# A linear-attention and feed-forward kernel: one-piece state update, operand sums shared with GpSimd, a second burst for Gram and query products

## The chip, the cores and the metric

The kernel runs on one core of a Trainium2 chip. The metric is the device time of one execution in microseconds (us); smaller is better. PE is TensorE (matrix products), DVE is VectorE, ACT is ScalarE, POOL is GpSimd, SP is SyncE. All data is float32.

## The reference

Two parts follow each other. The first is a delta-rule recurrence over 768 tokens, for 4 batches of 8 heads with 48 dimensions each; the second is a feed-forward layer on its output, seen as 3072 tokens of 384 features.

```python
k_n = k / (norm(k) + 1e-6)
state = 0                                   # 48 x 48 for each batch and head
for t in range(768):
    y[t] = q[t] @ state
    v_old = state.T @ k_n[t]
    state = state + beta[t] * outer(k_n[t], v[t] - v_old)
x = y.transpose(0, 2, 1, 3).reshape(3072, 384)
h = x @ w_in                                # 384 x 2048
g = maximum(h, 0) + alpha * minimum(h, 0)
out = g @ w_out                             # 2048 x 384
```

## The kernel before, in words

**Attention.** The tokens are cut into 12 chunks of C = 64 (NCH = 12), the batches into two pairs, which gives N = 24 steps n, one for a chunk and a pair of batches. Within a chunk the recurrence becomes a triangular system: the Gram products of the keys (`grams`, L527 and the DVE work L535 behind it) make the matrix, DVE eliminates in small blocks (`eliminate`, L606 and L612, for four steps at a time), PE combines the blocks (`between`, L788 and L800), `solve` (L958, then u at L962 on DVE) gives u of a step, `outputs` (L971) adds to its y, `query` (L836, copied at L840 by ACT) prepares the products of queries and keys, and `next_state` updates the state. `next_state` (L981 to L1001) writes its product for the two heads of a pair at rows 0 to 47 and 64 to 111 of a PSUM bank; DVE subtracts them from the state at L995, in two operations of 48 rows. For the first steps (n < 8, with exceptions) there is a form of 128 rows, one operation. Gram products run 9 steps ahead of the step that needs them, query products one step ahead. `to_ffn` (L1003) turns y by PE transposes and ACT copies it to `xt` (L1014), the input of the feed-forward part.

**Feed-forward.** It works on chunks of 256 tokens, 12 of them. Chunks 0 and 1 are ordinary products. For chunk 2 the second product, and from chunk 3 on both, take a form of Strassen's scheme with seven half-size products instead of eight, for which sums of the operands are made ahead:

- `input_sums` (L1260 to L1272, GpSimd) makes sums of w_in once; `token_sums` (L1295 to L1306, DVE, four operations of 128 x 128) makes sums of the chunk's tokens, needed by its first products at L1360.
- `ffn_in_fast` (from L1310) runs the first product in 8 groups of two blocks. For each group `common` (L1373) ends the shared products, ACT copies them to `sums` (L1379), GpSimd makes three additions (L1384), DVE adds the group's own products (`total`, L1388, writes `act`), ACT applies the negative branch (L1394, L1397) and DVE adds it (L1401 or L1404).
- `operand_sums` (L1061 to L1071, DVE) makes from `act` the four operand sums of the second product, for the first four groups (`first`) and the last four (`rest`): s1 and s2, then a21 (in place in `act`), then s4. A count of the matrix products issued (class `Due`, L1274) sets where in the order each of them comes. In chunks 3 to 7 (`some` in the code, c < ALL = 8) they are due late, some of them during the second product.
- `ffn_out_faster` (from L1459) runs the second product, p[0] to p[6] in PE's order (L1484), with additions into `o_sb` by DVE (L1480). `ffn_out_fast` is the same for chunk 2.

The feed-forward of chunk c can start when attention steps 2c and 2c + 1 are done; it is the filling between the attention's small products from step 6 on.

**Order.** The order of instructions on each engine is the program's order (L203); there is no scheduler behind it. From step n = JOINED = 6, each step has three stretches (L2082). In a stretch, first a burst of small attention products is issued at once; then the generators of the stretch are interleaved by their shares (`weave`): some 12 pieces of feed-forward, pieces of elimination, and a list `later` of what is left of the burst. `later` is spread over the part of the stretch that is left from a share `soon` on (0.5 is the second half). The three stretches begin with

1. `burst_a` (L1576): outputs and state update of step n - 1, the product of step n's queries or keys with the state;
2. `turn_round` (L1620): `to_ffn` of step n - 1, and at every second step `token_sums` of the next feed-forward chunk (L1626), and transposes for later steps;
3. `burst_b` (L1604): `solve(n)`, the Gram products of step n + 9, the query products of step n + 1 and the block products of `between`, all in one burst on PE, with the work on their results on DVE and ACT behind it.

Constants of the conditions: EARLY = 8, LATE = 16 (from there no Gram products are left), ASK = 8, SOME = 3, NJ = 4; `ends` is true where n % 4 == 2, when an elimination has to be ended.

Of the kernel before, what the change touches and what calls it, by code (L numbers as in the profile page):

```python
# [32 lines left out]
C = 64  # L33
# [12 lines left out]
def kernel(  # L46
# [62 lines left out]
    def dims(i):  # L109
        return slice(64 * i, 64 * i + D)  # L110
# [870 lines left out]
    def next_state(n, p=None):  # L981
        c, bp = steps[n]
        pieces, wide = [], n < 2 * NJ and n not in late_keys
        if c < NCH - 1:
            p = region(p, G * D, g=G)
            for g, a, t in quarters():
                nc.tensor.matmul(
                    p[half(a) if wide else dims(a), t, g], late_key(n)[half(t ^ a), 2 * g + a, 0 : C if wide else D],
                    us[n][half(t ^ a), a, g],
                )  # L990


            def less(rows):
                x = state[bp][rows]
                nc.vector.tensor_tensor(out=x, in0=x, in1=p[rows], op=ALU.subtract)  # L995

            if wide:
                pieces = [lambda: less(slice(0, 2 * C))]
            else:
                pieces = [lambda: less(dims(0)), lambda: less(dims(1))]  # L1000
        return pieces  # L1001

    def to_ffn(n, p=None):  # L1003
# [54 lines left out]
            i, flat = i - 6, more.rearrange("p i s e -> p (i s e)")  # L1058
        return flat[:, i * 512 : (i + 1) * 512].rearrange("p (f i) -> p f i", f=2)

    def operand_sums(b):  # L1061

        x = act[:, 4 * b : 4 * b + 4].rearrange("p i f (u e) -> p i f u e", u=2)
        a11, a12, a21, a22 = x[:, :, 0, 0], x[:, :, 1, 0], x[:, :, 0, 1], x[:, :, 1, 1]
        s1, s2, s4 = (sums[:, 4 * b : 4 * b + 4, i] for i in range(3))
        for dst, x, y, op in (
            (s1, a21, a22, ALU.add), (s2, s1, a11, ALU.subtract), (a21, a11, a21, ALU.subtract),
            (s4, a12, s2, ALU.subtract),
        ):
            nc.vector.tensor_tensor(out=dst, in0=x, in1=y, op=op)  # L1070
            yield  # L1071

    w_half = w_out.rearrange("p (i f) (v e) -> p i f v e", f=2, v=2)
# [95 lines left out]
    def ffn_out_fast(c):  # L1169
# [53 lines left out]
        add(o[0][:, right_], o[0][:, right_], p)  # L1223
        store(c, 0, o[0])
        yield
        p = yield from product(operand(1, 1), w_sum_(3))
        add(o[1][:, left], u[1], p)
        store(c, 1, o[1])
# [81 lines left out]
    def ffn_in_fast(c):  # L1310
# [97 lines left out]

            return own, common, total, below, slope

        first, rest = operand_sums(0), operand_sums(1)
        two_z = [beyond_sums[:, :, 1], beyond_sums[:, :, 2]]

        def run(gen):
# [44 lines left out]
    def ffn_out_faster(c):  # L1459
# [52 lines left out]
        last = c == NCH - 1  # L1512
        if last:
            store(c, 0, o[0], left)
        yield from some(p[6], sum_(2), weight(1, 1), range(FP - 2))
        assert c + 1 == NCH or c + 1 in whole
        yield from some(p[6], sum_(2), weight(1, 1), range(FP - 2, FP))
        add(o[0][:, right_], o[0][:, right_], p[6])
        store(c, 0, o[0], right_ if last else slice(0, DM))
# [84 lines left out]
    def burst_b(n):  # L1604

        b, x = ps_big(), ps_big()
        soon = solve(n, b[:, :, 0:WY])
        gram = grams(n + EARLY + 1, x[:, :, 0 : G * C])
        asked = query(n + 1, x[:, :, G * C : G * C + WY]) if n + 1 >= ASK else []
        wanted = [(n + 1, True, b[:, :, WY : WY + G * HB])]  # L1610
        if n > JOINED:
            wanted.append((n + 2, False, b[:, :, 2 * WY : 2 * WY + G * HB]))
        soon += between(*wanted)
        if n >= LATE:
            now(soon[:1])
            return soon[1:] + asked
        now(soon + gram[:2] + asked)
        return gram[2:] + [lambda: (squares if n < ONE else squared)(n + EARLY + 2)]

    def turn_round(n):  # L1620

        after = n > ASK and n % 2 == 1
        if n > JOINED and not after:
            to_ffn(n - 1)
            if n >= 2 * SOME + 2:
                token_sums(n // 2 - 1)  # L1626
        flips(n + EARLY + 1, n + 2)
        later = weigh(n + EARLY + 1)
        if after:
            later.append(lambda: to_ffn(n - 1))  # L1630
        load_next(n)
        load_q(n + 3)
        return later
# [472 lines left out]
    for n in range(JOINED, N):  # L2106
# [26 lines left out]
        if n == JOINED:  # L2133
            stretch(fill[2], blocks, share[2], later, *extra[2])
            for _ in blocks:
                assert False
            place(n + 2, (0,))
            place(n + 3, (0,))
            blocks = eliminate(m)
        else:  # L2140
            if ends:
                blocks = eliminate(m) if m < N // NJ else iter(())
            after = [(placing(n + 2, (1, 2, 3)), PLACING)]
            if n % NJ != 1:
                after.append((placing(n + 3, (0,)), 1))
            if n >= LATE:
                put_off, after = after, []
            stretch(
                fill[2], blocks, share[2], later, *after, *extra[2], soon=0.1 if n >= LATE or ends else 0.5
            )  # L2150
    stretch(12, iter(()), 0, burst_a(N))
    to_ffn(N - 1)
    token_sums(NCH - 1)
    for _ in tail:
        pass

# [29 lines left out]
```

## Time and profile before

| what | value |
|---|---|
| time, median of 3 runs | 649.26 us |
| the three runs | 650.35, 647.86, 649.26 us |
| time of the profiled execution | 649.88 us |
| its span in the profile | 648.1 us |
| mean granted clock of TensorE | 0.995 of full |
| stretch of the feed-forward chunks 3 to 7 in the trace | 220 to 470 us |

In the page's rows of engines, each engine's busy time is given with its share of the span and its count of instructions; PEld is the loading of weights, which lies beside PE's work. The chain of waits (fourth part) follows the work that ended last back to its start and gives shares of the span. In a row of the timeline stand the start, the duration (both us), the engine, the line, the operation, the tiles (out<-in), the shape and the number of instructions in the row; what is in brackets behind is the idle time of the engine ahead of it and what ended it. In a row of the windows stand the stretch and its length, then busy time with its count of instructions for PE, PEld, DVE, ACT and POOL, then three figures: the granted clock, the busy share of the DMA engines and their rate in GB/s. In a row of the waits stand the waiting instruction, its releaser, the sum of idle time, the count and the longest.

### The profile page before, as it was taken

Reading aid. Unit: us, or ns where it says so; the run is one execution under the profiler, and the core shown is the slowest. Engines: PE = TensorE matmul, PEld = TensorE weight load, DVE = VectorE, ACT = ScalarE, POOL = GpSimd, SP = SyncE. Lnnn points to the kernel's source line nnn. Section 1 sums busy time; section 2 is a strip of 40 time slices with the busy share of each in tenths; the row PEclk is TensorE's granted clock in tenths of the full one; section 3 lists DMA queues with packets and bytes.
Section 4 is the critical chain, followed back from the end, with each engine's and each line's share of the span. In section 5 each row is a group of like instructions: output and inputs, shape, how many; then the busy total and the mean of one; then the engine's idle time right before and its main releaser. Section 6 shows DMA issues by size and latency. Waiting matters only on the chain.

```text
span 648.1 us, 22180 instructions
## 1 busy us (share of the span) xinstructions
PE 631.2 (97%) x9387; PEld 566.5 (87%) x9387; DVE 500.5 (77%) x1182; ACT 307.2 (47%) x710; POOL 200.8 (31%) x377
## 2 busy tenths in 40 slices
PE   8989999999999999999999999999999999999997
PEld 7777777566889989999898989999999999999997
DVE  5868689978998799678969849969958568467383
ACT  6776754245554286287178167157145055042240
POOL 7267610010071241152051044044044053062360
PEclk9999999999999999999999989999999999999999
DMA  8756965113301320311311201121111210100000
GB/s 129 199 152 162 253 141 128 24 28 67 71 16 26 75 50 3 74 33 22 64 33 31 47 24 34 25 50 27 33 45 27 47 31 2 34 17 2 26 1 24
DMA packets 106803, 36.93 MB, mean 57 GB/s; under 512 B 99872, under 2 KB 103088, under 8 KB 106704
## 3 DMA queue, kind: packets, MB, share of 16 engines
q1 hardware_dynamic: 104832, 35.03, 25.0%
q8 instruction: 73, 1.20, 0.8%
q10 hardware_dynamic: 1872, 0.49, 0.4%
q14 instruction: 26, 0.21, 0.1%
HBM read 30.78 MB, written 4.72 MB: 55 GB/s over the span
## 4 chain that ended last, share of the span: by engine, by line
PE 71%; DVE 15%; issue 7%; ACT 3%; DMA 2%; POOL 1%; DVEq 0%; POOLq 0%; ACTq 0%
PE p_more L1484 12%; PE p_ffn L1484 8%; PE p_more L1360 5%; PE p_ffn L1159 5%; PE p_ffn L1350 4%; PE p_more L1350 4%; PE p_ffn L1116 3%; PE p_ffn L1355 3%; PE p_ffn L1181 3%; PE p_more L1355 3%; PE p_ffn L1360 3%; PE p_pair L788 2%; DVE prod L606 2%; PE p_pair L848 2%; PE p_pair L471 2%
## 5 line engine op out<-in xcount | busy, mean ns | idle before, releaser
L1384 POOL TENSOR_TENSOR sums<-sums 128x128 f32<-128x128 f32 (+1 forms) x201 | 119.8, 598 | 291.2 <-ACT sums L1379 280.5
L1116 PE MATMUL p_ffn<-xt,w_in 128*128 128x256 f32 x288 | 69.7, 389 | 2.1 <-ACT act L1126 1.2
L1116 PEld LDWEIGHTS p_ffn<-xt,w_in 128*128 128x128 f32 x288 | 52.2, 190 | 11.0 <-ACT act L1126 1.6
L1014 ACT COPY xt<-p_pair 128x384 f32<-128x384 f32 x22 | 10.4, 476 | 105.5 <-PE p_pair L1010 81.6
L612 DVE TENSOR_TENSOR block<-block,prod 128x30 f32<-128x30 f32 (+9 forms) x150 | 52.7, 351 | 5.2
L606 DVE TENSOR_TENSOR prod<-block 128x30 f32<-128x30 f32 (+9 forms) x150 | 51.9, 346 | 4.5 <-POOL block L596 2.7
L1484 PE MATMUL p_more<-w_out,act 128*128 128x192 f32 x288 | 52.1, 329 | 0.0
L1484 PEld LDWEIGHTS p_more<-w_out,act 128*128 128x128 f32 x288 | 47.0, 190 | 0.4
L1379 ACT COPY sums<-p_more 128x512 f32<-128x512 f32 x44 | 25.7, 583 | 40.3 <-PE p_more L1360 37.3
L1350 PE MATMUL p_ffn<-xt,w_in 128*128 128x256 f32 x140 | 43.2, 391 | 0.1
L1350 PE MATMUL p_more<-xt,w_in 128*128 128x256 f32 x128 | 38.9, 386 | 2.1 <-DVE act L1388 2.1
L962 DVE TENSOR_TENSOR u<-p_pair,wgt 128x384 f32<-128x384 f32 x20 | 11.1, 554 | 35.1 <-PE p_pair L788 35.1
L800 ACT COPY inv<-p_pair 32x256 f32<-32x256 f32 x40 | 14.5, 362 | 34.1 <-DVE u L962 33.3
L1388 DVE TENSOR_TENSOR act<-p_ffn,sums 128x512 f32<-128x512 f32 x35 | 23.8, 681 | 7.0 <-POOL sums L1384 3.5
L1379 ACT COPY sums<-p_ffn 128x512 f32<-128x512 f32 x23 | 13.4, 582 | 33.4 <-PE p_ffn L1360 33.1
L1394 ACT ACTIVATE a_t<-act 128x512 f32<-128x512 f32 x31 | 19.5, 631 | 17.3 <-DVE act L1388 17.1
L460 POOL TENSOR_TENSOR beta_t<-beta_t,rec 128x8 f32<-128x8 f32 x20 | 5.1, 254 | 72.4 <-DVE rec L454 65.8
L1388 DVE TENSOR_TENSOR act<-p_more,sums 128x512 f32<-128x512 f32 x32 | 21.7, 679 | 6.7 <-POOL sums L1384 6.5
L1484 PE MATMUL p_ffn<-w_out,act 128*128 128x192 f32 x144 | 26.4, 326 | 0.0
L1484 PE MATMUL p_more<-w_out,sums 128*128 128x192 f32 x144 | 24.9, 326 | 0.0
L1484 PEld LDWEIGHTS p_ffn<-w_out,act 128*128 128x128 f32 x144 | 23.9, 190 | 0.0
L1355 PEld LDWEIGHTS p_ffn<-xt,w_in 128*128 128x128 f32 x140 | 21.6, 195 | 1.9
(327 smaller groups left out, 1698.3 us busy)
## 6 DMA issues: line engine op xcount, KB each, us to landing
v_raw<-in_v_dram SPq DMA_DIRECT2D x48, 96.0 KB, 2.8
qp<-in_q_dram SPq DMA_DIRECT2D x48, 96.0 KB, 2.9
out_dram<-o_sb SPq DMA_DIRECT2D x90, 48.0 KB, 1.6
space_out<-in_moe_w_out_dram SPq DMA_DIRECT2D x11, 384.0 KB, 4.1
ke<-in_k_dram SPq DMA_DIRECT2D x43, 96.0 KB, 3.2
kl<-in_k_dram SPq DMA_DIRECT2D x80, 48.0 KB, 2.5
w_out<-in_moe_w_in_dram SPq DMA_DIRECT2D x6, 512.0 KB, 4.6
w_out<-in_moe_w_out_dram SPq DMA_DIRECT2D x5, 384.0 KB, 4.1
```

What stands on the lines that cost most here:

```text
L606: nc.vector.tensor_tensor(out=prod, in0=r[:, 0:j, j : j + 1].to_broadcast([128, j, n]), in1=r[:, j : j + 1, j + 1 : HB].to_broadcast([128, ...
L612: nc.vector.tensor_tensor(out=r[:, 0:j, j + 1 : HB], in0=r[:, 0:j, j + 1 : HB], in1=prod, op=ALU.add)
L1116: nc.tensor.matmul(p_h[:, i], w_in[:, t, (f + i) * 128 : (f + i + 1) * 128], xt[:, t], start=(t == 0), stop=(t == KT - 1),)
L1159: nc.tensor.matmul(p_o[u], gs[f // 2][:, f % 2, u * 128 : (u + 1) * 128], w_out[:, f], start=(f == 0), stop=(f == FT - 1),)
L1350: nc.tensor.matmul(p[:, f * 256 : f * 256 + 256], w(2, f), xt[:, 2], start=True, stop=False)
L1355: nc.tensor.matmul(p[:, j * 128 : j * 128 + 128], a, b, start=False, stop=(j > 0))
L1360: nc.tensor.matmul(q[:, j], a, b, start=True, stop=True)
L1379: nc.scalar.copy(z, q)
L1384: nc.gpsimd.tensor_tensor(out=dst, in0=a, in1=b, op=ALU.add)
L1388: nc.vector.tensor_tensor(out=g.rearrange("p f (u e) -> p (f u) e", u=2), in0=p.rearrange("p (i e) -> p i e", e=128), in1=z, op=ALU.add,)
L1394: nc.scalar.activation(r, g, ACT.Relu, scale=-1.0)
L1484: nc.tensor.matmul(p, x(i), w(i), start=(i == 0), stop=(i == FP - 1))
```

## The change

1. `next_state`: one subtraction over rows 0 to 111 instead of two over 48 rows. Rows 48 to 63 between the two heads are subtracted too; nothing reads them.
2. `operand_sums`: in chunks 3 to 7 the last two of four sums (a21 and s4), of `first` and of `rest`, go to GpSimd. There are 20 such operations.
3. `token_sums` of the next chunk is issued in the second product: in `ffn_out_fast` ahead of the last product, in `ffn_out_faster` behind the two additions of p[5], ahead of p[6]. It is taken out of `turn_round` and out of the end.
4. `burst_b`: for n = 8 to 14 the Gram products and the query products leave the burst and are issued as a burst of their own, as the first piece of `later`. For n from 16 on no Gram product was or is issued.
5. The share from which `later` is spread in the third stretch: 0.0 instead of 0.1 where `ends` and n is 8 to 15, 0.1 instead of 0.5 for the other n from 8 to 15.

Compared instruction by instruction, PE's order differs by the 7 places where 16 + 16 small products (L527 and L836) move behind some large ones; DVE's 16 pairs of state updates become 16 single ones and its 20 sums go to POOL; the token sums stand earlier or later by some instructions; on ACT some copies (L840, L572, L427, L741) change places; SP's order is the same.

```diff
@@ next_state
-                pieces = [lambda: less(dims(0)), lambda: less(dims(1))]
+                pieces = [lambda: less(slice(0, C + D))]
@@ operand_sums
-    def operand_sums(b):
+    def operand_sums(b, engine=nc.vector):
...
-        for dst, x, y, op in (
+        for i, (dst, x, y, op) in enumerate((
             (s1, a21, a22, ALU.add), (s2, s1, a11, ALU.subtract), (a21, a11, a21, ALU.subtract),
             (s4, a12, s2, ALU.subtract),
-        ):
-            nc.vector.tensor_tensor(out=dst, in0=x, in1=y, op=op)
+        )):
+            (nc.vector if i < 2 else engine).tensor_tensor(out=dst, in0=x, in1=y, op=op)
             yield
@@ ffn_out_fast
         yield
+        assert c + 1 in whole
+        token_sums(c + 1)
         p = yield from product(operand(1, 1), w_sum_(3))
@@ ffn_in_fast
-        first, rest = operand_sums(0), operand_sums(1)
+        engine = nc.gpsimd if some else nc.vector
+        first, rest = operand_sums(0, engine), operand_sums(1, engine)
@@ ffn_out_faster
+        if not last:
+            assert c + 1 in whole
+            token_sums(c + 1)
         yield from some(p[6], sum_(2), weight(1, 1), range(FP - 2))
@@ burst_b
-        gram = grams(n + EARLY + 1, x[:, :, 0 : G * C])
-        asked = query(n + 1, x[:, :, G * C : G * C + WY]) if n + 1 >= ASK else []
...
+        if ASK <= n < LATE - 1:
+
+            def second():
+                gram, asked = other()
+                rest[:] = gram[2:]
+                now(gram[:2] + asked)
+
+            rest = []
+            now(soon + between(*wanted))
+            return [second, lambda: now(rest), lambda: squared(n + EARLY + 2)]
+
+        gram, asked = other()
@@ turn_round
             to_ffn(n - 1)
-            if n >= 2 * SOME + 2:
-                token_sums(n // 2 - 1)
@@ the loop over the steps
-                fill[2], blocks, share[2], later, *after, *extra[2], soon=0.1 if n >= LATE or ends else 0.5
+                fill[2], blocks, share[2], later, *after, *extra[2], soon=0.0 if ends and ASK <= n < LATE else 0.1 if n >= ASK or ends else 0.5
             )
     stretch(12, iter(()), 0, burst_a(N))
     to_ffn(N - 1)
-    token_sums(NCH - 1)
```

`other()` makes the Gram products (for n below 16) and the query products (for n from 7 on) as before.

More of the change, by code (lines that the diff above doesn't have):

```diff
@@ L1514, in ffn_out_faster @@
             store(c, 0, o[0], left)
+        if not last:
+            assert c + 1 in whole
+            token_sums(c + 1)
         yield from some(p[6], sum_(2), weight(1, 1), range(FP - 2))
-        assert c + 1 == NCH or c + 1 in whole
         yield from some(p[6], sum_(2), weight(1, 1), range(FP - 2, FP))
@@ L1612, in burst_b, with other @@
             wanted.append((n + 2, False, b[:, :, 2 * WY : 2 * WY + G * HB]))
+        def other():
+            gram = grams(n + EARLY + 1, x[:, :, 0 : G * C]) if n < LATE else []
+            asked = query(n + 1, x[:, :, G * C : G * C + WY]) if n + 1 >= ASK else []
+            return gram, asked
+        if ASK <= n < LATE - 1:
[7 more added lines that the diff above has]
+        gram, asked = other()
         soon += between(*wanted)
```

## The prediction

> **What bounds the kernel now.** I read the first and fourth part of the page, then the waits of PE over 216 to 648 us, then the timeline at each of them.
>
> ```profile
> span 648.1 us, 22180 instructions
> PE 631.2 (97%) x9387; PEld 566.5 (87%) x9387; DVE 500.5 (77%) x1182; ACT 307.2 (47%) x710; POOL 200.8 (31%) x377
> PE 71%; DVE 15%; issue 7%; ACT 3%; DMA 2%; POOL 1%; DVEq 0%; POOLq 0%; ACTq 0%
> ```
>
> ```profile
> PE p_more L1350 <- DVE act L1388: 2.1, 2, 1.3
> ```
>
> PE is busy in 97% of the span. The change takes no matrix product away, so PE's 631 us of work stay; it can gain only by shortening waits. In the 432 us that it touches, PE waits for DVE in the two places of this row and once at a seam between chunks, and once for no partner that the profile shows. The timeline has the four, the idle time in brackets (1.28 + 1.24 + 0.86 = 3.4 us behind DVE):
>
> ```profile
> 242.59 0.70 PE L1350 MATMUL p_more<-xt,w_in 128*128 128x256 f32 x2 [1.28 <-DVE act L1388]
> 321.34 0.46 PE L1360 MATMUL p_ffn<-xt,w_in 128*128 128x128 f32 x2 [1.24 <-DVE o_sb L1480]
> 343.14 0.70 PE L1350 MATMUL p_more<-xt,w_in 128*128 128x256 f32 x2 [0.86 <-DVE act L1388]
> 378.54 0.25 PE L788 MATMUL p_pair<-diag,right 32*32 32x32 f32 x3 [1.39 <-issue]
> ```
>
> Two lie in the input products of chunks 3 and 5, one at the seam between chunks 4 and 5. Behind the fourth the granted clock falls (the third figure from the end of each row):
>
> ```profile
> 378.00:380.00 2.00, 1.46 (x12) 1.42 (x12) 1.18 (x4) 0.57 (x2) 0.00 (x0) 0.89 0.03 8
> 380.00:382.00 2.00, 2.00 (x9) 1.73 (x8) 0.64 (x2) 1.95 (x6) 0.00 (x0) 0.50 0.00 0
> 382.00:384.00 2.00, 2.00 (x13) 1.90 (x12) 0.53 (x1) 1.94 (x6) 1.17 (x3) 0.76 0.00 0
> ```
>
> The lost clock is 2 x 0.11 + 2 x 0.50 + 2 x 0.24 = 1.7 us, so this stall costs 3.1 us in all; nothing in the change touches it.
>
> **The state update.** Two subtractions of 48 rows become one of 112 rows. The trace has the pair and a one-piece form of 128 rows:
>
> ```profile
> 189.78 0.54 DVE L995 TENSOR_TENSOR beside<-beside,p_pair 128x384 f32<-128x384 f32 x1
> 259.51 1.11 DVE L995 TENSOR_TENSOR beside<-beside,p_pair 48x384 f32<-48x384 f32 x2
> ```
>
> So each of 16 updates frees 0.57 us of DVE. What that is worth at the waits comes below.
>
> **Two of four operand sums on GpSimd.** In chunks 3 to 7, four L1070 operations a chunk leave DVE. Each is 0.68 us long and 0.60 us from its start to the next one's:
>
> ```profile
> 252.56 0.68 DVE L1070 TENSOR_TENSOR sums<-sums,act 128x512 f32<-128x512 f32 x1
> 253.16 0.33 DVE L606 TENSOR_TENSOR prod<-block 128x168 f32<-128x168 f32 x1
> ```
>
> DVE is rid of 4 x 0.60 = 2.4 us a chunk. GpSimd needs 1.3 us for such an operation, and the two engines hold each other up:
>
> ```profile
> 178.56 1.27 POOL L1272 TENSOR_TENSOR ke<-w_in 128x512 f32<-128x512 f32 x1
> 179.91 1.32 POOL L1272 TENSOR_TENSOR ke<-ke,w_in 128x512 f32<-128x512 f32 x1
> 181.20 2.04 POOL L1272 TENSOR_TENSOR qp<-w_in 128x512 f32<-128x512 f32 x1
> ```
>
> ```profile
> 179.24 0.64 DVE L606 TENSOR_TENSOR prod<-block 128x30 f32<-128x30 f32 x1
> 179.92 0.21 DVE L612 TENSOR_TENSOR block<-block,prod 128x30 f32<-128x30 f32 x1
> 180.04 0.55 DVE L962 TENSOR_TENSOR u<-p_pair,wgt 128x384 f32<-128x384 f32 x1
> 181.16 0.95 DVE L1103 TENSOR_TENSOR w_out<-w_out,space_out 128x768 f32<-128x768 f32 x1
> ```
>
> L606 takes 0.64 us, against 0.21 for its twin L612 just behind, and ends when GpSimd's first operation does. L962, with one operand in PSUM, passes unhindered. L1103 came first, and GpSimd's third operation took 2.04 us. So whoever starts first goes through, and the other waits if DVE reads both operands from SBUF.
>
> The Trainium skill, "SBUF — State Buffer", section "Who interferes with whom", speaks against this edit: a DVE instruction with two SBUF inputs and a GpSimd instruction that reads SBUF exclude each other for a whole instruction, and issue order decides who blocks. The trace agrees (0.64 against 0.21 us). By that rule alone a moved sum may cost DVE its whole length; that is the slower rival.
>
> DVE's own business there is elimination (L606, L612), both operands in SBUF, each waiting for the one before, so that GpSimd slips in between; and three of the four moved operations become ready behind one another. Let D be how much later DVE reaches the end of a chunk. If GpSimd blocks nothing, D = -2.4 - 0.6 = -3.0 us. If each blocks its full 1.3 us, D = 5.2 - 3.0 = +2.2 us. I take 1.1 us each (the first runs partly beside additions with a PSUM operand), near the row of 0.64, which lost the whole rest: D = 4.5 - 3.0 = +1.5 us.
>
> GpSimd's queue bears it: its next work, the first L1384 of the following chunk, comes after 26.62 us of idleness (the two small L460 and L461 stand ahead of it).
>
> ```profile
> 272.73 1.79 POOL L1384 TENSOR_TENSOR sums<-sums 128x128 f32<-128x128 f32 x3 [26.62 <-ACT sums L1379]
> 261.93 1.46 PE L1484 MATMUL p_ffn<-space_out,act 128*128 128x192 f32 x8
> 268.33 2.77 PE L1484 MATMUL p_more<-w_out,sums 128*128 128x192 f32 x16
> ```
>
> PE reads the moved results from 261.93 (act) and 268.33 us on (sums). The last input of GpSimd's chain, the L1070 of 252.56, is there at 253.2. Three operations of 1.3 us, with DVE's 0.7 us between, are through by 259.2: hidden, with 2.7 us to spare. Without that cover, a late result would stall PE one for one.
>
> **The token sums**, moved behind the two additions that free PE's bank. At the seam of chunk 4:
>
> ```profile
> 319.58 0.28 DVE L1306 TENSOR_TENSOR sums<-xt 128x128 f32<-128x128 f32 x1
> 320.58 0.61 DVE L1480 TENSOR_TENSOR o_sb<-u,p_ffn 128x192 f32<-128x192 f32 x2
> 321.63 0.39 PE L1360 MATMUL p_ffn<-sums,ke 128*128 128x128 f32 x2
> ```
>
> PE's first product of the next chunk needs the bank (free at 321.19), its second the second token sum. In the new order the additions run at 319.58 + D, the second sum ends at 320.77 + D, and that second product starts 0.15 us later, at 320.92 + D, against 321.63: the stall changes by D - 0.7, at best by -1.24. Behind the additions on DVE wait only these sums and transposes. The seam of chunk 6 has little room too:
>
> ```profile
> 420.36 0.29 DVE L1306 TENSOR_TENSOR sums<-xt 128x128 f32<-128x128 f32 x1
> 422.55 0.39 PE L1360 MATMUL p_ffn<-sums,ke 128*128 128x128 f32 x2
> ```
>
> There the second product could start at 420.36 + 1.34 + D = 421.70 + D against 422.55: D - 0.85, at best 0. At D = 1.5 the seams cost 0.8 + 0.65 = **+1.5 us** (bounds: -1.2 at D = -3.0, +2.9 at +2.2). The seams of 3, 5 and 7 I cost at nothing, by that of 3:
>
> ```profile
> 268.17 0.29 DVE L1306 TENSOR_TENSOR sums<-xt 128x128 f32<-128x128 f32 x1 [0.54 <-ACT xt L1014]
> 270.93 0.38 PE L1360 MATMUL p_ffn<-xt,w_in 128*128 128x128 f32 x2
> ```
>
> DVE idles there for 0.54 us before the token sums; with the additions behind them (1.0 + 0.6 us) it is through at 269.8, 1.1 us ahead of PE.
>
> **The waits of 242.59 and 343.14** end with an L1388 (241.87, below) in a DVE stretch without gaps, and each has one shortened state update ahead of it. At most 0.57 us each comes through; part is lost because ACT and GpSimd work ahead of the same L1388. I take 0.45 each, **-0.9 us** (bounds: 0, and -2.1 if both waits go).
>
> ```profile
> 241.87 0.67 DVE L1388 TENSOR_TENSOR act<-p_more,sums 128x512 f32<-128x512 f32 x1
> 240.00:242.00 2.00, 1.32 (x10) 1.05 (x8) 1.97 (x5) 1.97 (x6) 0.63 (x1) 1.00 0.75 133
> ```
>
> **A second burst.** For n = 8 to 14, Gram and query products move behind the other small ones, after a few large products: seven more changes between large and small tiles. The old burst:
>
> ```profile
> 223.22 0.39 PE L1360 MATMUL p_ffn<-sums,ke 128*128 128x128 f32 x2
> 223.53 0.68 PE L958 MATMUL p_pair<-r,inv 64*64 64x48 f32 x32
> 224.03 0.66 PE L527 MATMUL p_pair<-k_t 48*64 48x64 f32 x32
> 225.76 0.49 PE L1360 MATMUL p_more<-xt,w_in 128*128 128x128 f32 x2
> 586.83 0.68 PE L958 MATMUL p_pair<-r,inv 64*64 64x48 f32 x32
> 587.44 0.76 PE L1484 MATMUL p_more<-w_out,act 128*128 128x192 f32 x3
> ```
>
> Products like 223.22 follow each other every 0.22 us, so entering costs 223.53 - 223.44 = 0.1 us. The same 32 small products take 0.50 us inside the burst (223.53 to 224.03) and 0.61 us when large ones follow (586.83 to 587.44): leaving costs 0.1 us more than going on. An additional burst is thus 0.2 us, 7 x 0.2 = **+1.4 us** (bounds: 0.5 if the seams inside the old burst, now gone, pay most of it; 2.8 at twice the price). In return u (L962) is released about 1 us earlier; the L535 that need the Gram product still hold DVE until the second burst ends, so I cost this at nothing. The ACT copies that move (L572, L840, L427) stand in another order ahead of the same L1379, with the same sum within 0.3 us. The share that starts pieces earlier (0.0, 0.1 for 0.5) only makes these moves; no DMA changes place on its queue.
>
> **Sum.** The profiled execution took 649.88 us (span 648.1 and 1.8 around it), 0.62 above the median 649.26. +1.5 - 0.9 + 1.4 = +2.0 gives 651.9 on its account, and **651.2 us** beside the median.
>
> **Rivals.**
>
> *DVE first at the port, faster.* With D = -2 or less the stall of 321.34 goes (-1.24), and 242.59 and 343.14 go with it (-2.1); the bursts cost 0.5 to 1.4. 649.88 - 3.3 + 1.0 = 647.6, 647.0 beside the median. For it: L1103 at 181.16. Against it: L606 at 179.24.
>
> *GpSimd blocks DVE in full, slower.* D = +2.2: seams +2.9, bursts +1.4, nothing gained in the input products: 654.2 on the profile's account. A seam stall of 1.24 + 1.5 = 2.7 us is twice the one that halved the clock; another 1.7 us would give 655.9. In the middle, and beside the median: 654.4 us. It decides against the change from D of about 1.6 us (seams 1.65 + bursts 1.4 - 0.9 = 2.2) on, past 0.5% from D of about 2. For it: the two-operand rows. Against it: DVE has PSUM work to put beside.
>
> The Trainium skill, "TensorE: Matmul & The Clock Gate", section "Why this matters for your kernels", lets the clock fall only after idle gaps of about 3 us; here it fell to 0.50 after 1.39 us, and not after 1.28, so length alone does not settle it. By that page the slower rival would stay without the extra 1.7 us.
>
> *The stall of 378.54 is not tied to this code.* It waits for nothing shown; if it falls elsewhere or away, the forecast loses up to 3.1 us: 648.1 beside the median. For it: the three runs before span 647.86 to 650.35.
>
> *The edits do not reach PE.* If DVE's relief and GpSimd's blocking cancel (D near 0.7), only the bursts show: 650.1.
>
> **How the numbers follow.** Forecast 651.2 (649 to 652.5) 0.40; edits that do not reach PE, 0.08; DVE first, 0.16; stall moved, 0.08; GpSimd blocks in full, 0.28. About 0.5% (3.25 us: 646.0 to 652.5) is what a measurement can tell here. Faster by more needs DVE first together with the stall gone, or the cheap bound of the bursts: 0.14. Slower by more: the blocking rival and a tail of the forecast: 0.32. Within: 0.54. The range runs from 646.0 to 655.5.
>
> **What would show it.** The state update as one row of about 0.54 us; L1070 on POOL at 1.3 us or more, DVE's L606 and L612 beside them at 1 us and above (right) or unchanged (DVE first). At the seams of chunks 4 and 6, PE L1360 waiting for L1306 or L1480, by 2 and 0.7 us. Waits for L1388 near 242 and 343 shorter by half. Two bursts where one was, 0.2 us dearer. I am wrong if the seams have no waits, if PE waits for POOL's sums, or if the clock falls at another place.

## The result and the profile after

The changed kernel took 646.00 us (median of 20 runs) against 649.41 us (20 runs of the kernel before, beside it): ratio 0.9951, 95% interval 0.9938 to 0.9963. That is 3.4 us faster, where I had forecast 1.9 us slower. First the page of the changed kernel: the span, the engines and the chain.

```profile
span 643.8 us, 22168 instructions
PE 628.3 (98%) x9387; PEld 562.4 (87%) x9387; DVE 503.5 (78%) x1146; ACT 307.0 (48%) x710; POOL 228.2 (35%) x397
PE 79%; DVE 11%; ACT 3%; issue 2%; DMA 2%; POOL 2%; SPq 0%; ACTq 0%; POOLq 0%; DVEq 0%
```

PE has the same 9387 products. It is busy 2.9 us less all the same, against the prediction's "PE's 631 us of work stay": in the profiled run of before the granted clock fell to one half twice, for 3.4 us each (in the first 20 us, and behind the stall of 378.54), and products take longer then (a pair of L1350 1.06 us in place of 0.60); in that of after it did not fall. DVE is busy 3.0 us longer, though 36 of its operations are gone (20 sums, and one of each pair of 16 updates). In the chain, DVE falls from 15 to 11% and "issue" from 7 to 2%. PE's waits over 216 to 660 us in the changed kernel (waiting instruction, releaser, sum, count, longest):

```profile
PE p_more L1352 <- DVE act L1390: 0.8, 1, 0.8
PE p_pair L788 <- ACT diag L766: 0.5, 2, 0.2
```

Of the four places of before, one is left with 0.8 us of its 1.28 (lines are 2 or 3 higher in the changed kernel: L1390 is the old L1388). The seam between chunks 4 and 5 has no wait, with the bank's additions early enough (DVE, then PE):

```profile
318.83 0.61 DVE L1483 TENSOR_TENSOR o_sb<-u,p_ffn 128x192 f32<-128x192 f32 x2
319.36 0.28 DVE L1308 TENSOR_TENSOR sums<-xt 128x128 f32<-128x128 f32 x1
```

```profile
319.97 0.38 PE L1362 MATMUL p_ffn<-xt,w_in 128*128 128x128 f32 x2
320.19 0.39 PE L1362 MATMUL p_ffn<-sums,ke 128*128 128x128 f32 x2
```

Not all of the profiles' difference (648.1 against 643.8) is the change's. 0.85 us of it lies ahead of 209 us, where no instruction has been changed; the clock fell at the start of the one profiled run and not of the other (first 20 us, before, then after; the clock is the third figure from the end):

```profile
0.00:20.00 20.00, 17.17 (x249) 14.96 (x250) 12.86 (x44) 13.38 (x39) 13.93 (x55) 0.91 0.85 149
```

```profile
0.00:20.00 20.00, 16.01 (x256) 12.50 (x257) 12.74 (x45) 13.49 (x40) 13.83 (x55) 1.00 0.75 136
```

So I compare the traces from 209 us on, by a mark that each attention step has: the start on PE of the small products of L971. The table has the mark's time in the kernel before, and how much later (+) or earlier it stands in others, with the offset at 209 us taken off. e1, e2, e4, e9, e10 and e16 are experiments, below.

```
mark in before   after    e1      e2      e4      e9      e10     e16
209.15            0.00   0.00    0.00    0.00    0.00    0.00    0.00
230.81           +0.34   0.00    0.00   +0.34    0.00    0.00    0.00
257.47           -0.18  -0.69    0.00   +0.45    0.00   +0.01   -0.67
281.62           +0.61  -0.69   +0.14   +1.20    0.00   +0.01   -0.67
306.47           +0.88  -0.76   +0.12   +1.47   -0.01    0.00   -0.75
332.10           -0.25  -2.08   +2.02   +0.84   -0.03   +1.24   -2.07
358.01           -0.79  -2.11   +2.02   +0.96   -0.03   +2.94   -2.11
385.42           -3.05  -3.91   +0.34   -1.07   -2.59   -0.32   -5.37
432.55           -3.05  -3.92   +3.06   -1.07   -2.51   +0.48   -5.37
503.96           -3.55  -4.10   +2.74   -1.34   -2.51   +0.48   -5.56
```

The changed kernel loses where nothing else happens (the first row with a number, +0.34, is a second burst) and gains in three places: around 242 us, at the seam of 321 us, and most, 2.3 us net, between 358 and 385 us; 0.5 us more come behind 433 us. The largest is the stall of which the prediction says that nothing in the change touches it.

### The profile page after: what moved, and what is told of

Its sections match the earlier page's. It is cut to its first block, busy times and chain, and to the rows that moved or that the text cites. A ratio compares the mean times of both kernels' runs of the same rounds, so it can differ in the third digit from the quotient of the medians.

```text
span 643.8 us, 22168 instructions
## 1 busy us (share of the span) xinstructions
PE 628.3 (98%) x9387; PEld 562.4 (87%) x9387; DVE 503.5 (78%) x1146; ACT 307.0 (48%) x710; POOL 228.2 (35%) x397
## 4 chain that ended last, share of the span: by engine, by line
PE 79%; DVE 11%; ACT 3%; issue 2%; DMA 2%; POOL 2%; SPq 0%; ACTq 0%; POOLq 0%; DVEq 0%
PE p_more L1487 15%; PE p_ffn L1487 11%; PE p_more L1362 6%; PE p_ffn L1159 5%; PE p_ffn L1352 4%; PE p_ffn L1116 4%; PE p_more L1352 4%; PE p_ffn L1357 3%; PE p_ffn L1362 3%; PE p_more L1357 3%; PE p_ffn L1181 3%; PE p_pair L788 2%; PE p_ffn L1326 2%; PE p_pair L848 2%; PE p_pair L471 2%
## 5 line engine op out<-in xcount | busy, mean ns | idle before, releaser
L612 DVE TENSOR_TENSOR block<-block,prod 128x30 f32<-128x30 f32 (+9 forms) x150 | 60.7, 405 | 5.2
L1116 PEld LDWEIGHTS p_ffn<-xt,w_in 128*128 128x128 f32 x288 | 52.2, 190 | 10.9 <-ACT act L1126 2.1
L606 DVE TENSOR_TENSOR prod<-block 128x30 f32<-128x30 f32 (+9 forms) x150 | 54.5, 363 | 4.6 <-POOL block L596 2.7
L1487 PE MATMUL p_more<-w_out,act 128*128 128x192 f32 x288 | 52.9, 330 | 0.0
L1487 PEld LDWEIGHTS p_more<-w_out,act 128*128 128x128 f32 x288 | 46.9, 190 | 0.6
L1390 DVE TENSOR_TENSOR act<-p_ffn,sums 128x512 f32<-128x512 f32 x35 | 23.8, 681 | 5.9 <-PE p_ffn L1357 3.3
L1390 DVE TENSOR_TENSOR act<-p_more,sums 128x512 f32<-128x512 f32 x32 | 21.7, 677 | 6.5 <-POOL sums L1386 6.5
L1487 PE MATMUL p_ffn<-w_out,act 128*128 128x192 f32 x144 | 26.3, 326 | 0.0
L1487 PE MATMUL p_more<-w_out,sums 128*128 128x192 f32 x144 | 24.9, 326 | 0.0
L1070 DVE TENSOR_TENSOR sums<-sums,act 128x512 f32<-128x512 f32 x20 | 24.5, 1223 | 0.1
L1487 PEld LDWEIGHTS p_ffn<-w_out,act 128*128 128x128 f32 x144 | 23.9, 190 | 0.0
```

What stands on the lines that cost most here:

```text
L606: nc.vector.tensor_tensor(out=prod, in0=r[:, 0:j, j : j + 1].to_broadcast([128, j, n]), in1=r[:, j : j + 1, j + 1 : HB].to_broadcast([128, ...
L612: nc.vector.tensor_tensor(out=r[:, 0:j, j + 1 : HB], in0=r[:, 0:j, j + 1 : HB], in1=prod, op=ALU.add)
L1070: (nc.vector if i < 2 else engine).tensor_tensor(out=dst, in0=x, in1=y, op=op)
L1116: nc.tensor.matmul(p_h[:, i], w_in[:, t, (f + i) * 128 : (f + i + 1) * 128], xt[:, t], start=(t == 0), stop=(t == KT - 1),)
L1390: nc.vector.tensor_tensor(out=g.rearrange("p f (u e) -> p (f u) e", u=2), in0=p.rearrange("p (i e) -> p i e", e=128), in1=z, op=ALU.add,)
```

## The experiments

Theories. **D**: DVE reaches the ends of the chunks earlier against PE than I had worked out, by the state update, by the second burst, or because GpSimd costs it less. **Stall**: the stall of 378.54 belongs to the old burst. Rival to both: no single part does it, or chance. "Part k" is the k-th item of the list of the change. All ratios are to the kernel before, run beside on the same chip.

### One part alone: e1 to e4

```diff
# e1: part 1 alone
-                pieces = [lambda: less(dims(0)), lambda: less(dims(1))]
+                pieces = [lambda: less(slice(0, C + D))]
# e2: part 2 alone
+            (nc.vector if i < 2 else engine).tensor_tensor(out=dst, in0=x, in1=y, op=op)
# e3: part 3 alone
-                token_sums(n // 2 - 1)
# and token_sums(c + 1) ahead of p[6]
# e4: parts 4 and 5 alone
+            return [second, lambda: now(rest), lambda: squared(n + EARLY + 2)]
```

> Only the state update as one operation of 112 rows; all else as before. Theory 'DVE is early': what gained is DVE's place ahead of PE, so 0.57 us less per step shortens the waits behind L1388 (1.28 and 0.86 us) by about 0.5 each and that at the seam of chunk 4 to 5 (1.24 us) by 0.6 to 1.1: 1.5 to 2 us faster. Rival 'order of the seam and bursts': under 0.5 us, waits unchanged. Theory 'chance stall' (the stall of 378.54 and its clock loss, 3.1 us, come and go without the change): it may be absent here; 'tied to the old burst': it is here, since the old burst is.

> Only two of four operand sums on GpSimd in chunks 3 to 7. Theory 'GpSimd blocks for about 1.05 us each' (as the profile of the changed kernel shows for L612 and L1070 on DVE): D = 4 x 1.05 - 2.4 = +1.8 us at a chunk's end, the seam wait of chunk 4 to 5 grows from 1.24 to about 3 us and the seam of chunk 6 gets one of about 1: 2 to 3 us slower. Rival 'the sums are where the gain is': DVE's end of chunk earlier, 1 to 2 us faster.

> Only the token sums behind the two additions of the second product. Theory 'order of the seam': the wait at the seam of chunk 4 to 5 goes from 1.24 to about 0.5 us, nothing else moves: 0.7 us faster. Rival 'no effect by itself': the wait only changes its name (from L1480 to L1306) with the same 1.2 us: within 0.3 us.

> Only the second burst for Gram and query products, with its earlier start of the pieces. Forecast as given: 7 x 0.2 = 1.4 us slower, waits unchanged. Rival 'the second burst puts DVE ahead': u and the L1388 behind it run 1 to 2 us earlier against PE, the waits for L1388 (1.28 and 0.86) and the seam's 1.24 go in part: 0.5 to 1.5 us faster in spite of the 1.4. The stall of 378.54 lies in the old burst: gone here if tied to it.

Measured: **e1** 645.51 us, ratio 0.9933 (0.9914 to 0.9952); **e2** 653.68 us, 1.0057 (1.0039 to 1.0075); **e3** 648.92 us, 0.9982 (0.9968 to 0.9996); **e4** 649.25 us, 0.9995 (0.9979 to 1.0011). The smallest edit, one line, carries as much as the whole change. The waits of PE behind 216 us, e1 first, then e2, then e4 (from 210 us on):

```profile
PE p_more L1350 <- DVE act L1388: 1.8, 2, 0.9
PE p_pair L788 <- issue: 1.2, 1, 1.2
PE p_pair L788 <- ACT diag L766: 0.2, 1, 0.2
```

```profile
PE p_ffn L1360 <- DVE o_sb L1481: 4.3, 2, 2.1
PE p_more L1350 <- DVE act L1388: 1.8, 2, 1.0
PE p_pair L788 <- issue: 1.4, 1, 1.4
PE p_pair L471 <- DVE a_t L549: 0.8, 1, 0.8
PE p_ffn L1350 <- DVE act L1388: 0.4, 1, 0.4
```

```profile
PE p_more L1350 <- DVE act L1388: 1.6, 2, 1.0
PE p_pair L788 <- ACT diag L766: 0.4, 2, 0.2
PE p_ffn L1360 <- DVE o_sb L1480: 0.3, 1, 0.3
PE p_pair L836 <- issue: 0.2, 1, 0.2
```

e1 has no wait at a seam any more; its 4.1 us by the table (4.4 by time) are more than the 1.5 to 2 expected, and 1.8 of them lie between 358 and 385 us, where its stall stays (1.25 us) but the clock does not fall. e2 has two waits at seams, of 2.1 us each (about 3 and 1 expected): the blocking that I forecast is real, and alone it makes the kernel slower. e3 does what its theory said (the seam's wait goes from 1.24 to 0.2 us, and the clock still falls behind the stall). In e4 the stall of 1.4 us without a releaser is a wait of 0.2 us at L836, at a seam 0.3 us are left of 1.24, and yet the time of its 12 runs is that of before (by its one trace, 1.3 us are gained from 209 us on): the burst pays for most or all of what it wins.

### All but one part: e5 to e8

```diff
# e5: the whole change without part 1
-                pieces = [lambda: less(slice(0, C + D))]
+                pieces = [lambda: less(dims(0)), lambda: less(dims(1))]
# e6: without part 2
-            (nc.vector if i < 2 else engine).tensor_tensor(out=dst, in0=x, in1=y, op=op)
+            nc.vector.tensor_tensor(out=dst, in0=x, in1=y, op=op)
# e7: without part 3: token_sums in turn_round again
# e8: without parts 4 and 5: burst_b and soon as before
```

> The whole change but with the state update in two operations of 48 rows as before. Theory 'the state update carries the gain': DVE is 0.57 us later per step, 1.14 by the end of a chunk, so the seams that lie free by about 0.5 to 1 us get waits and those for L1388 grow: 1.5 to 3 us slower than the changed kernel, about as before. Rival 'any part will do': within 0.5 us of the changed kernel.

> The whole change but all four operand sums on DVE. Theory 'GpSimd's sums cost DVE 4 x 1.05 - 2.4 = 1.8 us a chunk, but the other parts leave DVE that much room': same time as the changed kernel, within 1 us, no wait at a seam. Rival 'the sums help in company': 1 us or more slower than the changed kernel. Rival 'they still cost PE': 1 us or more faster.

> The whole change but token sums as before, ahead of the additions. DVE then frees the bank 0.7 to 1 us later at each seam. The profile of the changed kernel has the additions end 0.5 us ahead of PE at the seam of chunk 4 to 5, so a wait of about 0.3 there and perhaps one at chunk 6 to 7: 0.3 to 1 us slower than the changed kernel. Rival 'no effect': within 0.3 us.

> The whole change but Gram and query products in the old burst, pieces with the old share. Theory 'the stall of 378.54 belongs to the old burst': it comes back (1.2 to 1.5 us without a releaser) while seven changes between large and small products (1.4 us) go: within 1 us of the changed kernel. Rival 'the second burst puts DVE ahead': the waits for L1388 and at the seams come back, 2 to 3 us slower than the changed kernel.

Measured: **e5** 649.90 us, 1.0012 (0.9998 to 1.0027); **e6** 646.07 us, 0.9953 (0.9936 to 0.9969); **e7** 647.89 us, 0.9977 (0.9960 to 0.9994); **e8** 647.38 us, 0.9967 (0.9949 to 0.9986). Without the state update nothing is left of the gain. Without the GpSimd sums it stays whole: beside all the other parts they neither help nor harm. Without the new place of the token sums, e7, more goes than the 0.3 to 1 us expected: PE waits at two seams, and at 504 us its trace stands at -1.83, that of the changed kernel at -3.55:

```profile
PE p_ffn L1360 <- DVE o_sb L1481: 0.9, 2, 0.5
```

So this part carries about half of the gain in company. Without the second burst, e8, the trace stands at -2.46, 1.1 us behind the changed kernel (the intervals of the times overlap), and 1.6 us behind e1: beside the state update, but without the second burst, the GpSimd sums still cost. e8 brings the old burst back, and with it the stall, among the last L788 of the same burst (its timeline):

```profile
375.47 0.25 PE L788 MATMUL p_pair<-diag,right 32*32 32x32 f32 x4 [1.27 <-issue]
```

The stall is there in before, e1, e2, e3 and e8, which have the old burst, and not in after, e4, e5, e6 and e7, which have the new one (0.2 to 0.3 us at L836 in e4 and e7). It is not chance.

### What the stall is: e9 to e12

In the page of before, the instruction queue has this row; the view of DMAs for the 0.2 us from 375.8 has the start of one of its packets:

```profile
q8 instruction: 73, 1.20, 0.8%
```

```profile
q8 instruction: 1, 0.02, 39.2%
```

1.20 MB in 73 packets is 16.4 KB each. PE's 9387 products and 9387 weight loads make 257 instructions to a packet, and each record of a product has one of a weight load beside it. A burst with 16 products (32 records) each of L958, L527 and L836 and twice 32 records of L788 is 160 records of products, 320 instructions; the burst near 377 us begins at 374.88, and its last products start at 378.54, behind the stall. If PE's instructions come in blocks of 256, each asked for when the block before it is begun, a burst that holds a whole block runs dry at its end. The kernel's order can be left as it is, and the blocks moved against it, by leaving out or adding products at the very start:

```diff
# e9, and e11 and e12 too
-    identities(6, big[1][:, 0])
+    identities(3, big[1][:, 0])
# e10
     identities(6, big[1][:, 0])
+    short(12, big[1][:, 0])
# e11: with part 1; e12: with parts 1 and 3
```

> The kernel before, with 3 of the 6 warming products at its very start left out (their results are not used), so that every later PE instruction stands 12 places earlier in PE's stream. Theory 'instruction supply': the page has 73 packets on the instruction queue with 1.20 MB, and 2 x 9387 PE instructions, so 257 to a packet; the stall of 378.54 comes where PE has run through one such block inside one burst of some 320 instructions, three products before its end. 12 places earlier the block ends behind the burst: the stall and the clock loss behind it go, 1.4 to 3.1 us faster, with no other change behind 216 us. Rival 'chance or data': the stall stays at the same product, within 0.5 us.

> The kernel before, with 12 small products more at its start (48 PE instructions; PE waits there for the first inputs anyway). Theory 'instruction supply': by the counts of PE's records ahead of each burst, the blocks then end inside the bursts of 324.8, 347.8 and 374.9 us: three stalls of about 1.4 us in place of one, each sooner in the last (48 instructions earlier in its burst): 2.5 to 6 us slower than before. Rival 'chance or data': one stall at the same product, within 0.5 us.

> The state update as one operation, and 3 warming products fewer at the start; nothing else of the change. By the instruction supply the stall of about 1.3 us that the run with the state update alone kept goes as well: 1.2 us faster than that run, 2 us faster than the changed kernel. Rival: as the run with the state update alone.

> State update as one operation, token sums behind the additions, 3 warming products fewer at the start; the sums on DVE and one burst as before. The run with the state update alone had no wait at a seam any more, so the token sums find nothing to shorten: same as the run with the state update and 3 warming products fewer, within 0.5 us. Rival 'the token sums still help': 0.5 us or more faster.

Measured: **e9** 647.94 us, 0.9965 (0.9948 to 0.9982); **e10** 653.89 us, 1.0056 (1.0034 to 1.0077); **e11** 644.59 us, 0.9923 (0.9897 to 0.9949); **e12** 645.24 us, 0.9925 (0.9898 to 0.9953). The timeline of e9, then of e10:

```profile
377.58 0.28 PE L1360 MATMUL p_ffn<-sums,ke 128*128 128x128 f32 x1
378.41 0.27 PE L1360 MATMUL p_ffn<-sums,ke 128*128 128x128 f32 x1 [0.55 <-issue]
```

```profile
327.99 0.22 PE L788 MATMUL p_pair<-inv,mid 32*32 32x32 f32 x2 [1.08 <-issue]
352.67 0.25 PE L788 MATMUL p_pair<-diag,right 32*32 32x32 f32 x4 [1.47 <-issue]
```

Three products fewer (6 records of products and 6 of weight loads, 12 instructions) put the stall 12 instructions later in the program: behind the burst, among large products, where it is 0.55 us long. 48 instructions more put two stalls into the bursts of 324.8 and 347.8 us, where there had been none, and took the one of 377 away.

Two counts in the traces show that it is the supply. Counted with all that a trace holds for PE (its semaphore instructions too), the stall stands behind 11,969 instructions in every profile that has it near 377 us, whether 12 are left out at the start (e9, e11, e12) or none; the two of e10 stand behind 10,433 and 11,201, which is 6 x 256 and 3 x 256 fewer. And in each of these profiles the last packet of the instruction queue ahead of the stall ends 1.24 to 1.45 us before PE goes on (in before, it takes from 375.93 to 377.18, and PE goes on at 378.54). I had expected a third stall in e10; it did not come, since there the packet came from 376.07 to 377.21, ahead of the burst, which begins at 377.72. Why it was fetched that early is open.

e11 is 0.7 us faster than e1 by the ratios, which overlap, and not the 1.2 expected: behind the burst its stall, and that of e12, is still 0.97 us long.

The profiled run of e10 (span 648.5) lies at the lower edge of its runs (650.26 to 657.29), so the table above shows less of its loss than its median. e12, with nearly the ratio of e11, tells that beside the state update alone the token sums' new place gains nothing; beside the GpSimd sums it does (e7).

### Whether the clock falls behind it, and moving the blocks out of the way: e13 to e18

e13 to e15 are the kernel before, unchanged. The others leave out 10 of the 12 warming products at the start, 40 instructions:

```diff
-    identities(6, big[1][:, 0])
+    identities(2, big[1][:, 0])
...
-    identities(1, big[1][:, 0])
...
-    identities(3, big[0][:, 0])
...
-    identities(2, big[0][:, 0])
# e16: with part 1; e17: nothing else; e18: with the whole change
```

> The kernel before, unchanged, for a second profile. Theory 'instruction supply': a stall without releaser of 1.3 to 1.6 us at the same product (third from the end of the burst near 377 us). Open: whether the granted clock falls behind it as in the first profile; if by chance, it falls in some profiles and not in others.

> The kernel before, unchanged, for a third profile: the stall near 377 us at the same product; the clock behind it as in e13 or not.

> The kernel before, unchanged, for a fourth profile: the stall near 377 us at the same product; the clock behind it as in e13 or not.

> The state update as one operation, and 10 warming products fewer at the start (40 PE instructions). Theory 'instruction supply': every block now ends at least 35 instructions behind a burst, among large products, so no stall without releaser behind 216 us: about 1 us faster than with 3 fewer, if the start does not get slower for want of the warming products. Rival: the stall of 1.0 us stays.

> The kernel before with 10 warming products fewer at the start. Instruction supply: stall (1.2 to 1.5 us) and the clock loss behind it (1.7 us, in three of four profiles of the kernel before) go; the state update is as before: 2.5 to 4 us faster than before, with the waits for L1388 (1.0 and 0.9 us) and the seam's 1.2 us left. Rival 'the gain is in the start': 1.2 us faster, by the place of the first steps in the run with the state update and 10 fewer.

> The whole change with 10 warming products fewer. Its bursts hold no whole block, so behind 216 us nothing changes: same as the changed kernel within 0.5 us if the start is neutral, 1.2 us faster if the start gains.

The stall came in all three (e13, e14, e15):

```profile
380.78 0.25 PE L788 MATMUL p_pair<-diag,right 32*32 32x32 f32 x3 [1.43 <-issue]
```

```profile
380.55 0.25 PE L788 MATMUL p_pair<-diag,right 32*32 32x32 f32 x3 [1.20 <-issue]
```

```profile
382.19 0.25 PE L788 MATMUL p_pair<-diag,right 32*32 32x32 f32 x3 [1.49 <-issue]
```

Behind it the clock fell in e13 and e15 and stayed in e14; the windows of 378 to 386 us in e13, then e14:

```profile
378.00:386.00 8.00, 6.57 (x140) 6.14 (x131) 2.11 (x5) 4.30 (x12) 2.42 (x6) 0.79 0.02 4
```

```profile
378.00:386.00 8.00, 6.80 (x165) 6.28 (x156) 2.34 (x5) 4.54 (x13) 2.64 (x6) 1.00 0.02 4
```

**e16** took 643.59 us, 0.9894 (0.9874 to 0.9914), the fastest of all; **e17** 647.66 us, 0.9953 (0.9936 to 0.9970); **e18** 646.19 us, 0.9933 (0.9911 to 0.9955). The waits of e16 from 210 us on have no stall without a releaser:

```profile
PE p_more L1350 <- DVE act L1388: 1.8, 2, 0.9
PE p_pair L788 <- ACT diag L766: 0.2, 1, 0.2
```

From 209 to 504 us, e17 gains 2.43 us on the kernel before, e16 5.56 and e18 3.75, the changed kernel 3.55. So with the stall gone the state update is worth 3.1 us by the profiles. It is worth the same with the stall but without the loss of clock: e14 stands at -1.01 at 504 us, e1 at -4.10. And e18 shows the changed kernel indifferent to where the blocks lie. By time e18 is 0.9933 to the changed kernel's 0.9951; their intervals overlap, so a gain in the start is not shown.

## Why the prediction was wrong

Two steps failed. The stall was costed at nothing, since "nothing in the change touches it"; the second burst takes it away, which is worth 3.3 us between these two profiles. And D, from which the seams were costed, was taken as +1.5 us; it was -0.8, because the state update counts twice in a chunk and the second burst puts DVE ahead.

**The state update** was taken at half of what it gave. Its duration was right (one row of 0.55 us, here from the changed kernel):

```profile
283.48 0.55 DVE L995 TENSOR_TENSOR beside<-beside,p_pair 112x384 f32<-112x384 f32 x1
```

But the formula for D has 0.6 us for it, one update, where a chunk of the feed-forward spans two attention steps and DVE keeps what both free. The two rows that measure D are DVE's last L434 ahead of the seam of chunk 4 and PE's last products L1484 (L1487): 318.36 - 317.33 = 1.03 us in the kernel before. The rows of before, after, e1 and e8 (DVE and PE of each):

```profile
318.36 0.55 DVE L434 TENSOR_REDUCE norm<-ksq 128x8 f32<-128x384 f32 x1
317.33 2.77 PE L1484 MATMUL p_more<-w_out,sums 128*128 128x192 f32 x16
```

```profile
317.61 0.55 DVE L434 TENSOR_REDUCE norm<-ksq 128x8 f32<-128x384 f32 x1
317.37 2.77 PE L1487 MATMUL p_more<-w_out,sums 128*128 128x192 f32 x16
```

```profile
316.31 0.55 DVE L434 TENSOR_REDUCE norm<-ksq 128x8 f32<-128x384 f32 x1
316.60 2.77 PE L1484 MATMUL p_more<-w_out,sums 128*128 128x192 f32 x16
```

```profile
316.20 0.55 DVE L434 TENSOR_REDUCE norm<-ksq 128x8 f32<-128x384 f32 x1
314.56 2.77 PE L1487 MATMUL p_more<-w_out,sums 128*128 128x192 f32 x16
```

Behind the first pair that is 0.24, -0.29 and 1.64 us, so D = -0.8 in the changed kernel (forecast +1.5), -1.3 with the state update alone (two updates are 2 x 0.57 = 1.1), +0.6 with all but the burst. From -1.3 to +0.6 go GpSimd's sums, 1.9 us; from +0.6 to -0.8 the second burst, 1.4 us. All but the burst by the forecast's own working would have been +1.5; 0.7 of the difference to +0.6 is the second update.

**GpSimd's sums** were sized right. DVE's operation behind each is held up for most of a GpSimd operation; s2, which DVE does while GpSimd does a21, is the plain case: ten in chunks 3 to 7, before and after.

```profile
L1070 DVE TENSOR_TENSOR sums<-sums,act 128x512 f32<-128x512 f32 x10 | 6.8, 683 | 0.0
```

```profile
L1070 DVE TENSOR_TENSOR sums<-sums,act 128x512 f32<-128x512 f32 x10 | 17.6, 1758 | 0.0
```

1758 - 683 ns = 1.08 us each, against the 1.1 taken. Besides, four forms of L606 and L612 got 0.39 to 0.59 us longer, five times each, which is 1.0 us for each of the other ten sums, if it is put down to them. This is what "SBUF — State Buffer", section "Who interferes with whom", of the Trainium skill states, and e2 is what it costs. That 4 x 1.08 - 2.4 = 1.9 us a chunk did no harm in the changed kernel fits e6 and e8: the state update and the second burst had already put DVE that far ahead.

**The second burst** I costed at 0.2 us each and at nothing on DVE. On PE the first costs 0.34 us (table, 209 to 231 us), and those of 273 and 373 us have in addition a wait for ACT's `diag`, since the block products now come directly behind L958. On DVE the forecast said that the L535, which need the Gram product, hold it until the second burst ends. The profile of the kernel before and that of the changed one show it otherwise at 276 us:

```profile
276.68 0.56 DVE L962 TENSOR_TENSOR u<-p_pair,wgt 128x384 f32<-128x384 f32 x1 [4.54 <-PE p_pair L788]
277.16 0.41 DVE L535 TENSOR_TENSOR same<-p_pair,wgt 128x256 f32<-128x256 f32 x1
277.49 0.42 DVE L535 TENSOR_TENSOR right<-p_pair,wgt 128x256 f32<-128x256 f32 x1
277.82 0.68 DVE L1388 TENSOR_TENSOR act<-p_more,sums 128x512 f32<-128x512 f32 x1
```

```profile
275.17 0.56 DVE L962 TENSOR_TENSOR u<-p_pair,wgt 128x384 f32<-128x384 f32 x1 [4.05 <-PE p_pair L788]
275.65 0.68 DVE L1390 TENSOR_TENSOR act<-p_more,sums 128x512 f32<-128x512 f32 x1
276.99 0.42 DVE L535 TENSOR_TENSOR same<-p_pair,wgt 128x256 f32<-128x256 f32 x1 [0.66 <-PE p_pair L836]
```

The addition that PE and ACT wait for has changed places with the L535 and runs 2.17 us earlier (1.03 of it by PE's own lead at 257 us). The L535 wait, but in a gap that DVE had anyway.

**The seam and the token sums.** The formula, D - 0.7 and at best -1.24, held within 0.3 us; with D = -0.8 it gives -1.24, and the wait is gone. With D = +0.6, e8, it gives about -0.1, and the seam kept 0.85 of its 1.24, which is -0.4.

**The waits behind L1388** got 0.5 and 0.86 us shorter, 1.4 together (forecast 0.9, bounds 0 and 2.1). The second one needs two parts: 0.84 us of it are left in e1, 0.64 in e4, none where the state update and the second burst come together.

**The stall** was the step that failed outright. The second burst touches it, by putting large products between the small ones, so that a block of instructions lasts longer. In the changed kernel the supply runs short by only 0.2 us, which its timeline has as a longer L836 (0.85 us, where the others take 0.63). The step from 358 to 385 us is -2.26 us with a burst in it; a profile of the kernel before in which the clock did not fall (e14) passes it 1.85 us faster than the first one, so most of that step is the clock. My third rival had this (3.1 us, chance 0.08), as an accident.

The sum from 209 us on, by the traces: seam -1.2, waits behind L1388 -1.4, stall and clock -3.3 (1.58 us from start to start, and 1.7), makes -5.9; measured -3.55. The remainder of about +2.4 would be the second bursts, with their waits for `diag` and at L836 (forecast 1.4, bounds 0.5 to 2.8); it is not measured by itself, and the same working gives +3.4 for e4, where nothing but the bursts was changed. From the forecast of +2.0 to there, 2.7 us were missed at the seams, 0.5 behind L1388 and 3.3 at the stall, and 1.0 in the bursts the other way.

Three sums of the prediction's working are off, and none of them decides: 4 x 1.1 - 3.0 is 1.4 and not 1.5; three operations of 1.3 us and 0.7 us between, from 253.2 on, end at 257.8 and not at 259.2; and 649.26 with the bursts alone is 650.7 and not 650.1.

What stays open: why the clock falls behind one stall and not behind another. Behind the stall near 377 us it fell after 1.39 (first profile), 1.43 (e13), 1.45 (e3) and 1.49 us (e15), and not after 1.20 (e14), 1.25 (e1), 1.27 (e8) and 1.36 us (e2): at this place the longer four have the fall, the shorter four do not. But it did not fall behind the 1.47 us in another burst of e10, nor behind the 2.1 us that PE waits for DVE at the seam in e2 (clock 1.00 in the window behind it):

```profile
324.00:328.00 4.00, 4.00 (x66) 3.78 (x70) 1.53 (x6) 1.06 (x2) 2.00 (x5) 1.00 0.35 95
```

So length alone does not settle it. In the traces' records the clock changes at multiples of 3.41 us from each other; each of the eight stalls near 377 us lies within one such step, while that of e10 lies across two, with 1.30 us in the first. That would fit a bound between 1.36 and 1.39 us in one step, but the wait at e2's second seam, with 1.84 us in one step among 128x128 products, does not, and no run was made to vary it. "TensorE: Matmul & The Clock Gate", section "Why this matters for your kernels", of the Trainium skill speaks of gaps above about 3 us; three profiles of the kernel before show a fall behind half of that. In how many of e1's other runs the clock stayed up is not known.

## What to carry to other kernels

A lead or a lag of an engine adds up over the whole stretch up to the next point where the bound engine waits for it: count how many steps lie in the stretch before sizing an edit that sits in each of them. Price an edit that costs an engine time against the room that the others leave it: the same moved sums cost 3.8 us alone and nothing beside the state update and the second burst together. And treat a stall that has no releaser as part of the program, not as noise: look whether it stands at the same instruction in another run, and what the order of the instructions has to do with it.

## What the runs showed of the hardware

PE's instructions arrive in packets of some 256 (73 packets of 16.4 KB for 18,774 products and weight loads). In the profiles with a stall, 2.2 to 2.7 us pass from the start of such a packet until PE goes on behind it; a burst of 320 instructions takes 2.2 us where it has no stall (near 378 us in e10). Nine profiles have a stall of 1.1 to 1.5 us towards the end of such a burst. 12 instructions fewer at the start of the program, some 375 us earlier, move it behind the burst (0.55 us in e9, 0.97 in e11 and e12), and 40 fewer removed it. Ten warming products left out and one line for the state update make the version of this study with the lowest median, 643.59 us, 1.06% (0.86 to 1.26) below the kernel before, where the changed kernel is 0.49% (0.37 to 0.62) below.
